# Chunked attention with memory and an MLP on one core: moving the copies of memory rows from GpSimd to VectorE, and re-ordering the front

## The chip, the cores and the metric

One NeuronCore of a Trainium2 chip. The time is that of the device for one execution, in microseconds (us). The engines are named as in the profile: PE is TensorE (PEld its loading of weights), DVE is VectorE, ACT is ScalarE, POOL is GpSimd, SP is SyncE, which here only issues transfers. The kernel before takes 242.05 us (median of three runs, 241.57 to 242.69).

## The reference, cut to what matters

Four batches, eight heads, 768 positions, heads of 64. Queries come in chunks of 32; a chunk sees 16 keys to the left, its own 32, 8 to the right, and 8 memory keys. What comes out is normalised, goes through an MLP of 512 to 2048 to 512 with relu, and is added to itself.

```python
chunk, left_ctx, right_ctx = (32, 16, 8)
for c in range(nc):
    c_start = c * chunk; c_end = c_start + chunk
    l_start = max(0, c_start - left_ctx); r_end = min(S, c_end + right_ctx)
    k_full = np.concatenate([mem_k, k[:, :, l_start:r_end]], axis=2)
    v_full = np.concatenate([mem_v, v[:, :, l_start:r_end]], axis=2)
    scores = scale * np.matmul(q[:, :, c_start:c_end], k_full.transpose(0, 1, 3, 2))
    a = np.exp(scores - np.max(scores, axis=-1, keepdims=True))
    a = a / (np.sum(a, axis=-1, keepdims=True) + 1e-09)
    out[:, :, c_start:c_end] = np.matmul(a, v_full)
...                                   # x: out with the heads side by side, 512 wide
xn = (x - mu) / np.sqrt(var + 1e-06) * g_ln
return x + np.maximum(xn @ w_ch1, 0.0) @ w_ch2
```

## The kernel before

The work is cut into 24 tiles of 128 positions (six for each batch), and these into eight units of three tiles for the MLP. The order of all instructions is written by hand: a prologue, then a plan of 28 steps for each unit `u`. In steps 0 to 15 stands one `up` projection each, in 16 to 27 one part of a `down` projection each; `at(u, step, ...)` puts other work behind a step.

Values are kept in groups of 64 positions: `V` has 104 rows (96 of context, 8 of memory) for each of 12 groups, and two buffers for even and odd batches. The 8 memory rows are the same in every group, so they are copied within SBUF from `memv16`. Keys are kept transposed in `KT` in the same groups, with the memory keys as columns 96 to 103.

```python
att = [ps.tile([128, 2, 512], FP32, ...) for i in range(2)]   # PSUM, two banks each
mm = [ps.tile([128, 512], FP32, ...) for i in range(4)]       # PSUM, one bank each

def v_mem(b, g0, g1, eng):           # 8 rows, g1 - g0 groups of 640 elements
    src = memv16[96:W, b, :, :]
    copy(eng, free(V[b % 2][96:W, g0:g1, :, :], 0, [[H * VW, g1 - g0], [1, H * VW]]),
         bass.AP(tensor=src.tensor, offset=src.offset,
                 ap=[list(src.ap[0]), [0, g1 - g0], [1, H * VW]]))

def key_piece(b, src, g, first, lo, n, eng, half=None):   # PSUM -> KT, one group
    ...
def pieces(b, blk, banks, phase):
    for n in range(2):
        key_piece(b, banks[phase], 4 * blk + n, *PIECES[n], dve, phase)
        key_piece(b, banks[1 - phase], 4 * blk + 2 + n, *PIECES[2 + n], act, 1 - phase)

def turn_keys(b, blk):               # 8 transposes on PE, then the first pieces
    p = slot("att")
    banks = [as16(p[:, h, :]) for h in range(2)]
    block_slot[b, blk] = banks
    transpose_block(b, blk, 0, banks)
    pieces(b, blk, banks, 0)
def more_keys(b, blk):
    pieces(b, blk, block_slot[b, blk], 1)
    edges(b, blk, dve)
def turn_queries(b, blk):            # 8 transposes, two copies on ACT
    ...
def mix(b, blk, which, eng):         # re-orders a loaded block for the transposes
    ...
def cross(b, blk, which):            # batches 2 and 3: transposed by DMA instead of PE
    ...
    nc.sync.dma_start_transpose(out=o, in_=i)
def norm(b, t):                      # xn = (x - mean) * g
    nc.vector.scalar_tensor_tensor(out=xn[i % 4], in0=xs[i % 9], scalar=nmean[t], in1=gb, ...)
def turn_x(b, t):                    # transposes xn into xT: PE in units 0 and 1, then DMA
    ...
def up(u, hc, lo=0, n=3):            # 4 matmuls of 128x384 into one bank of mm, then a relu
    p = slot("mm")[:, 0 : 128 * n]
    ...
    relu(act if hc % 2 else dve, rT[c][:, i, 128 * lo : 128 * (lo + n)], p)
def up_tile(u, c, i, eng):           # the same for one tile: 16 matmuls of 128x128
    ...
```

The first block of keys and queries is loaded in fp32 and cast by VectorE and ScalarE (`mix_raw`); all other loads are issued by GpSimd and cast on the way. The prologue and the plan, as far as they are spoken of:

```python
for which in range(2):               # first block: keys, then queries
    for par in range(2):
        nc.sync.dma_start(out=raws[which][par], in_=dram((k, q)[which], ...))
nc.scalar.dma_start(out=memkf, in_=dram(mem_k, ...))
nc.scalar.dma_start(out=grow, in_=dram(moe_g_ln, ...))
load_mem_v(0, nc.scalar)
...
load_w1(1)
v_mem(0, 2, 6, pool)
load_block(0, 1, 1)
...
warm(6)                              # matmuls on zeros
p = slot("att")
nc.tensor.matmul(out=p[:, 0, :], lhsT=gone, rhs=grow, start=True, stop=True)  # gain, fp32
...
scores(0, 0)
v_mem(0, 0, 2, dve)
...
at(0, 13, v_mem, 0, 6, NG, pool)
at(1, 0, turn_keys, 1, 0)
at(1, 0, v_mem, 1, 0, 4, dve)
at(1, 1, more_keys, 1, 0)
at(1, 2, turn_queries, 1, 0)
at(1, 4, v_mem, 1, 4, NG, pool)
...
for b in (2, 3):
    for i in range(3):
        at(w, 8 + i, v_mem, b, 4 * i, 4 * i + 4, pool)
```

Of the kernel before, what the change touches and what calls it, by code (L numbers as in the profile page):

```python
# [15 lines left out]
def kernel(  # L16
# [80 lines left out]
    def as16(t):  # L97
        return t.bitcast(FP16)

    def copy(eng, out, in_):  # L100
        if eng is nc.scalar:
            eng.copy(out=out, in_=in_)  # L102
        else:
            eng.tensor_copy(out=out, in_=in_)  # L104
# [27 lines left out]

    def v_mem(b, g0, g1, eng):
# [39 lines left out]
    def key_piece(b, src, g, first, lo, n, eng, half=None):  # L173

        h, m = (0, 8) if half is None else (4 * half, 4)
        copy(eng, free(KT[b % 2], GW * g + 16 + 8 * lo + h, [[W, 4], [8, n], [1, m]]),
             free(src, 4 * (first + lo), [[1, 4], [4, n], [128, m]]))
# [16 lines left out]
            key_piece(b, banks[phase], 4 * blk + n, *PIECES[n], dve, phase)  # L194
            key_piece(b, banks[1 - phase], 4 * blk + 2 + n, *PIECES[2 + n], act, 1 - phase)

    def first_pieces(b, blk, banks, k0):

        for n in range(2):
            key_piece(b, banks[n], 4 * blk + k0, *PIECES[k0], dve, n)  # L200
            key_piece(b, banks[1 - n], 4 * blk + k0 + 1, *PIECES[k0 + 1], act, 1 - n)

    def edges(b, blk, eng):
        if blk:
# [11 lines left out]
            )  # L216

    def turn_keys(b, blk):
        p = slot("att")
        banks = [as16(p[:, h, :]) for h in range(2)]  # L220
        block_slot[b, blk] = banks
        transpose_block(b, blk, 0, banks)
        pieces(b, blk, banks, 0)
# [207 lines left out]


    raws = ((osb[0], osb[1]), (osb[2], xs[4]))
    for which in range(2):
        for par in range(2):
            nc.sync.dma_start(
                out=raws[which][par],
                in_=dram((k, q)[which], 4 * par * HS, [[512, 32], [HS, 4], [1, 512]]),
            )

    def load_mem_v(b, eng):
        eng.dma_start(
            out=xs[5 + b][96:W, :], in_=dram(mem_v, b * 4096, [[64, 8], [512, 8], [1, 64]])
        )

    nc.scalar.dma_start(out=memkf, in_=dram(mem_k, 0, [[64, 128], [128 * 64, 2], [1, 64]]))
    nc.scalar.dma_start(out=grow, in_=dram(moe_g_ln, 0, [[512, 1], [1, 512]]))
    load_mem_v(0, nc.scalar)

    PAIR = 1.0 / 128 + 15.0 / 2**20  # L450

    def ones(i, g0, g1, eng):

        eng.memset(V[i].bitcast(FP32)[:, g0:g1, :, 32:40], PAIR)
# [12 lines left out]
    def mem_vals(b):  # L467
        copy(act, memv16[96:W, b, :, 0:64], xs[5 + b][96:W, :].rearrange("p (h d) -> p h d", h=8))

    make_identity(nc, identity)  # L470
    nc.vector.memset(zero, 0.0)
    nc.vector.memset(gone, 1.0)
    ones(0, 0, 2, dve)
    nc.vector.memset(V[0][0:32, 0, :, :], 0.0)
    clear_keys(0, dve)
    nc.vector.memset(mhalf, -0.5)
    nc.vector.memset(memv16.bitcast(FP32)[96:W, :, :, 32:40], PAIR)
    ones(0, 2, NG, dve)
    copy(dve, memk16, memkf)
    total(band[:, 0:1], 56, 96)  # L480
    total(band[:, 1:2], 0, 32)
    total(cnt[:, 2:3], 88, 96)
    nc.vector.tensor_tensor(out=band[:, 1:2], in0=band[:, 1:2], in1=cnt[:, 2:3], op=ALU.add)
    nc.vector.tensor_scalar(out=band, in0=band, scalar1=NEG, scalar2=None, op0=ALU.mult)

    mem_vals(0)
    load_v(0, 0)
    load_v(0, 1)
    load_block(0, 1, 0)
# [1 line left out]
    load_v(0, 2)  # L491
    load_v(0, 3)
    load_w1(1)
    v_mem(0, 2, 6, pool)
    load_block(0, 1, 1)
    load_w1(2)
    load_v(0, 4)
# [8 lines left out]
    nc.gpsimd.memset(V[1][0:32, 0, :, :], 0.0)  # L506
    nc.gpsimd.memset(V[1][64:96, NG - 1, :, :], 0.0)
    load_block(0, 2, 1)
    load_w2(1)
    clear_keys(1, pool)  # L510
    load_v(0, 8)
    load_v(0, 9)
    load_w2(2)
    load_v(0, 10)
    load_v(0, 11)
    load_w2(3)

    warm(6)
    p = slot("att")
    nc.tensor.matmul(out=p[:, 0, :], lhsT=gone, rhs=grow, start=True, stop=True)  # L520
    gp = p
    mem_keys()
    warm(1)
    K0 = [as16(mm[0]), as16(mm[1])]
    Q0 = [as16(mm[2]), as16(mm[3])]
    mix_raw(0, raws[0], 0, dve)
    mix_raw(0, raws[0], 1, act)
    transpose_block(0, 0, 0, K0)
    mix_raw(1, raws[1], 0, dve)
    mix_raw(1, raws[1], 1, act)  # L530
    first_pieces(0, 0, K0, 0)
    transpose_block(0, 0, 1, Q0)
    mem_cols(0, dve)
    copy(act, gb, gp[:, 0, :])
    quarter_q(0, 0, 0, Q0)
    warm(1, 512, gp[:, 1, :])
    scores(0, 0)
    v_mem(0, 0, 2, dve)
    soften(0, 0, 0)
    soften(0, 0, 1)  # L540
    mix(0, 1, 0, dve)
    first_pieces(0, 0, K0, 2)
    quarter_q(0, 0, 1, Q0)
    transpose_block(0, 1, 0, K0)
    total(cnt[:, 0:1], 16, 128)
    count_v(0, 0, 0)
    values(0, 0)
    first_pieces(0, 1, K0, 0)
    key_right(0, 3, dve)
    norm(0, 0)  # L550
    scores(0, 1)
    soften(0, 1, 0)
    soften(0, 1, 1)
    warm(2, 512, mm[2])
    turn_x(0, 0)
    values(0, 1)
    turn["mm"] = 2
    up_tile(0, 0, 0, act)
    norm(0, 1)
    first_pieces(0, 1, K0, 2)  # L560
    key_left(0, 4, dve)
    mix(0, 1, 1, dve)
    up_tile(0, 1, 0, act)
    turn_x(0, 1)
    transpose_block(0, 1, 1, K0)
    quarter_q(0, 1, 0, K0)
    quarter_q(0, 1, 1, K0)
    up_tile(0, 0, 1, act)
    scores(0, 2)
    soften(0, 2, 0)  # L570
    up_tile(0, 1, 1, dve)
    soften(0, 2, 1)
# [3 lines left out]
    up_tile(0, 2, 0, dve)  # L576
    values(0, 2)
    up_tile(0, 2, 1, act)
    norm(0, 2)
    mix(0, 2, 0, dve)  # L580
    up_tile(0, 3, 0, act)
    up_tile(0, 3, 1, act)
    turn_x(0, 2)
    mix(0, 2, 1, dve)
    plan = {}

    def at(u, step, fn, *args):
# [34 lines left out]
        load_block(b, blk, 0)  # L622
        load_block(b, blk, 1)

    at(0, 13, v_mem, 0, 6, NG, pool)
    order = [(load_pair, (0,))] + [(load_v, (g,)) for g in range(4)]
    order += [(load_pair, (1,)), (mem_cols, (pool,)), (load_v, (4,)), (load_v, (5,))]
    order += [(load_pair, (2,))] + [(load_v, (g,)) for g in range(6, 12)]
# [3 lines left out]
    at(0, 26, count_v, 1, 1, NG - 1)  # L632
    at(0, 24, mix, 1, 0, 0, dve)
    at(0, 26, mix, 1, 0, 1, dve)
    at(1, 0, turn_keys, 1, 0)
    at(1, 0, v_mem, 1, 0, 4, dve)
    at(1, 1, more_keys, 1, 0)
    at(1, 2, mix, 1, 1, 0, dve)
    at(1, 2, turn_queries, 1, 0)
    attend(6, 3, 7, 1)  # L640
    at(1, 4, v_mem, 1, 4, NG, pool)
    at(1, 4, mix, 1, 1, 1, dve)
    at(1, 6, turn_keys, 1, 1)
    at(1, 7, more_keys, 1, 1)
    at(1, 9, turn_queries, 1, 1)
    attend(7, 9, 13, 1)
    attend(8, 12, 16, 1)
    at(1, 15, mix, 1, 2, 0, dve)
    at(1, 19, turn_keys, 1, 2)
    at(1, 20, more_keys, 1, 2)  # L650
    at(1, 20, mix, 1, 2, 1, dve)
    at(1, 23, turn_queries, 1, 2)

    for b in (2, 3):
        u = 2 * b - 1
        w = u - 1
        for blk in range(3):
            at(w - 1, 23 + blk, load_pair, b, blk)
        at(w, 0, mem_cols, b, pool)
        for g in range(NG):  # L660
            at(w, 1 + g // 2, load_v, b, g)
        for i in range(3):
            at(w, 8 + i, v_mem, b, 4 * i, 4 * i + 4, pool)
# [64 lines left out]
```

## Time and profile before

| what | measured |
|---|---|
| time, median of three runs | 242.05 us |
| span of the profiled execution | 241.3 us |
| PE busy | 217.1 us (90%) |
| DVE busy | 133.9 us (55%) |
| ACT busy | 105.7 us (44%) |
| POOL busy | 117.3 us (49%) |
| PE busy in 0 to 80 us | 60.8 us |
| mean granted clock of PE | 0.969 |

The page gives busy times for the whole span; with PE at 90% they don't say which part of the span could be shorter. For that it has a line for each engine in which each digit stands for a fortieth of the span (6 us), in tenths, and one for the clock granted to PE. A table of shorter stretches gives the same in us, with the number of instructions in brackets. The timeline lists instructions in order of time; in brackets it has how long the engine was idle before, and which instruction ended that idle time. Line numbers are those of the kernel; L104 is the copy helper, so all copies of VectorE and GpSimd bear it and are told apart by their tiles.

### The profile page before, as it was taken

How to read it: one execution, taken by the hardware profiler on the slowest of the kernel's cores; microseconds unless marked ns; L12 is line 12 of the kernel's file. 1: busy time of each engine (PE TensorE's matmuls, PEld its weight loads, DVE VectorE, ACT ScalarE, POOL GpSimd, SP SyncE). 2: the span in 40 equal slices, each digit the busy share in tenths (PEclk: the TensorE clock that was granted, in tenths of full speed). 3: DMA queues.
4: the chain of work that ended last, by engine and by line, in shares of the span. 5: the costliest groups of instructions: out<-in, count | busy, mean ns of one | idle time of the engine just before them, and what ended most of it. 6: DMA issues, size and time to landing. Idle time of an engine off the chain costs nothing.

```text
span 241.3 us, 4939 instructions
## 1 busy us (share of the span) xinstructions
PE 217.1 (90%) x1944; PEld 133.3 (55%) x1944; DVE 133.9 (55%) x320; ACT 105.7 (44%) x220; POOL 117.3 (49%) x173
## 2 busy tenths in 40 slices
PE   8557859899678999999999999997999999999993
PEld 2245758554445645664566457643674467446653
DVE  5656293249836663679657436773475257515221
ACT  3543521855155832773387207732674057203300
POOL 7987696998700077899401387699111101200000
PEclk9999995999959999999999999999999999999999
DMA  6999999999300169999951299999911311221012
GB/s 173 183 196 196 199 198 196 169 146 78 119 0 3 22 84 182 220 130 152 175 148 24 65 166 204 125 132 173 210 42 22 109 46 24 43 87 43 3 43 87
DMA packets 72857, 27.85 MB, mean 115 GB/s; under 512 B 60929, under 2 KB 68865, under 8 KB 72834
## 3 DMA queue, kind: packets, MB, share of 16 engines
q0 software_dynamic: 45632, 14.56, 58.5%
q1 hardware_dynamic: 26856, 12.90, 25.8%
q8 instruction: 15, 0.25, 0.4%
q10 hardware_dynamic: 346, 0.08, 0.2%
q14 instruction: 8, 0.07, 0.1%
HBM read 30.28 MB, written 6.29 MB: 152 GB/s over the span
## 4 chain that ended last, share of the span: by engine, by line
PE 67%; DMA 16%; POOL 8%; DVE 5%; issue 2%; ACT 1%; DVEq 0%
PE mm L366 30%; PE mm L392 27%; PE att L279 4%; DMA w2c<-in_moe_w_ch_dram 4%; DMA w1c<-in_moe_w_ch_dram 4%; DMA st<-in_q_dram 3%; DMA xT<-xn 3%; PE att L300 3%; POOL st L120 3%; POOL V L128 2%; PE mm L414 1%; DVE KT L104 1%; DVE V L104 1%; DMA V<-in_v_dram 1%; POOL V L104 1%
## 5 line engine op out<-in xcount | busy, mean ns | idle before, releaser
L392 PE MATMUL mm<-w2c,rT 128*128 128x512 f16 x368 | 82.6, 379 | 0.0
L366 PE MATMUL mm<-xT,w1c 128*128 128x384 f16 x448 | 80.2, 332 | 1.8 <-DMA xT<-xn 1.3
L366 PEld LDWEIGHTS <-w1c 128*128 128x128 f16 x448 | 49.3, 115 | 25.5 <-issue 2.5
L392 PEld LDWEIGHTS <-rT 128*128 128x128 f16 x368 | 34.9, 98 | 40.0
L360 DVE TENSOR_SCALAR rT<-mm 128x384 f16<-128x384 f32 (+1 forms) x60 | 33.9, 564 | 33.1 <-PE mm L366 28.2
L358 ACT ACTIVATE rT<-mm 128x384 f16<-128x384 f32 (+1 forms) x64 | 32.3, 505 | 42.1 <-PE mm L366 19.0
L289 ACT ACTIVATE AT<-att,band 104x512 f16<-104x512 f32 x48 | 31.3, 685 | 28.8 <-PE att L279 28.6
L331 POOL TENSOR_SCALAR veps<-sq 128x1 f32<-128x1 f32 x24 | 5.6, 235 | 73.4 <-ACT junk L325 40.1
L128 POOL DMA_DIRECT2D V<-in_v_dram x48 | 37.5, 786 | 7.5 <-issue 3.4
L401 DVE SCALAR_TENSOR_TENSOR osb<-mm,rstd,xs 128x512 f32<-128x512 f32 x23 | 17.2, 749 | 30.6 <-PE mm L392 28.3
L104 POOL COPY V<-memv 8x2560 f16<-8x2560 f16 (+2 forms) x9 | 25.4, 2842 | 0.9 <-DVE V L104 0.7
L325 ACT ACTIVATE junk<-xs,nmean 128x512 f16<-128x512 f32 x24 | 17.3, 720 | 12.9 <-DVE nmean L314 12.9
L320 DVE SCALAR_TENSOR_TENSOR xn<-xs,nmean,gb 128x512 f16<-128x512 f32 x24 | 22.1, 922 | 0.4
L279 PE MATMUL att<-QR,KT 64*104 64x64 f16 x384 | 16.5, 237 | 5.2 <-ACT QR L102 3.7
L279 PEld LDWEIGHTS <-KT 64*104 64x104 f16 x384 | 13.0, 137 | 9.2 <-issue 6.1
L308 DVE SCALAR_TENSOR_TENSOR xs<-att,rec 128x512 f32<-128x512 f32 x24 | 16.6, 692 | 0.8
L377 PE MATMUL mm<-xT,w1c 128*128 128x128 f16 x192 | 14.5, 242 | 2.6 <-ACT KT L102 1.2
L377 PEld LDWEIGHTS <-w1c 128*128 128x128 f16 x192 | 13.6, 122 | 3.1 <-issue 2.9
L335 POOL TENSOR_TENSOR rstd<-veps,mhalf 128x1 f32<-128x1 f32 x24 | 14.3, 597 | 2.0
L102 ACT COPY KT<-rawk 128x352 f16<-128x352 f16 (+1 forms) x12 | 8.8, 791 | 11.7 <-DMA rawk<-iv 11.7
L120 POOL DMA_DIRECT2D st<-in_k_dram x22 | 12.6, 590 | 2.0 <-DMA st<-in_k_dram 1.0
L120 POOL DMA_DIRECT2D st<-in_q_dram x22 | 12.4, 579 | 2.4 <-DMA st<-in_q_dram 1.3
(74 smaller groups left out, 146.6 us busy)
## 6 DMA issues: line engine op xcount, KB each, us to landing
out_dram<-osb SPq DMA_DIRECT2D x23, 256.0 KB, 2.1
V<-in_v_dram POOLq DMA_DIRECT2D x40, 96.0 KB, 8.1
st<-in_k_dram POOLq DMA_DIRECT2D x22, 128.0 KB, 5.9
st<-in_q_dram POOLq DMA_DIRECT2D x22, 128.0 KB, 6.5
w1c<-in_moe_w_ch_dram POOLq DMA_DIRECT2D x4, 512.0 KB, 9.4
w2c<-in_moe_w_ch_dram POOLq DMA_DIRECT2D x4, 512.0 KB, 9.2
V<-in_v_dram POOLq DMA_DIRECT2D x8, 80.0 KB, 7.4
osb<-in_k_dram SPq DMA_DIRECT2D x2, 256.0 KB, 3.5
```

Of the source, the lines that this page charges most:

```text
L104: eng.tensor_copy(out=out, in_=in_)
L120: nc.gpsimd.dma_start(out=s[:, 512 * par : 512 * par + 512], in_=dram((k, q)[which], (b * H + 4 * par) * HS + blk * 256 * D, [[512, 32], [ ...
L128: nc.gpsimd.dma_start(out=V[b % 2][lo:hi, g, :, 0:64], in_=dram(v, b * H * HS + (64 * g - 16 + lo) * D, [[64, hi - lo], [HS, H], [1, 64]]),)
L279: nc.tensor.matmul(out=p[0:W, par, (4 * gg + j) * 64 : (4 * gg + j) * 64 + 64], lhsT=KT[b % 2][rows, 2 * t + gg, j, :], rhs=free(QR[b % 2] ...
L289: nc.scalar.activation(out=free(AT[t % 3], 32 * c, [[64, 16], [1, 32]]), in_=free(p, 4 * c, [[64, 16], [1, 4], [8, 8]], W), func=ACTF.Exp, ...
L320: nc.vector.scalar_tensor_tensor(out=xn[i % 4], in0=xs[i % 9], scalar=nmean[t], in1=gb, op0=ALU.add, op1=ALU.mult,)
L325: nc.scalar.activation(out=junk, in_=xs[(NT * b + t) % 9], func=ACTF.Square, bias=nmean[t], scale=1.0, accum_out=sq[t],)
L358: nc.scalar.activation(out=o, in_=p, func=ACTF.Relu)
L360: nc.vector.tensor_scalar(out=o, in0=p, scalar1=0.0, scalar2=None, op0=ALU.max)
L366: nc.tensor.matmul(out=p, lhsT=free(w1c[c][:, dt, :], i, [[4, 128]]), rhs=xT[u % 2][:, dt, 128 * lo : 128 * (lo + n)], start=(dt == 0), st ...
L377: nc.tensor.matmul(out=p[:, 128 * k_ : 128 * k_ + 128], lhsT=free(w1c[c][:, dt, :], k_, [[4, 128]]), rhs=xT[u % 2][:, dt, 128 * i : 128 * ...
L392: nc.tensor.matmul(out=p, lhsT=rT[c][:, k_, 128 * i : 128 * i + 128], rhs=w2c[c][:, k_, :], start=(c == 0 and k_ == 0), stop=(c == 3 and k ...
```

## The change

It has four parts.

1. The memory rows of values of batches 0 and 1 are copied by VectorE, in pieces of two or four groups at places of their own; GpSimd copies those of batches 2 and 3 as before. In return GpSimd clears and fills the constant columns of the first V buffer ahead of its first loads.
2. The two transfers of the first queries are issued by ScalarE's queue, beside those of the keys on SyncE's. The small transfers (memory keys, gain, memory values) move to SyncE's queue, behind the keys.
3. `turn_keys` transposes into two of the four one-bank tiles instead of one two-bank tile.
4. The front is re-ordered: the gain's matmul comes after the first scores, the pieces of keys of the first two blocks are written one group at a time, projections of ready tiles stand earlier; a few steps of the plan shift, among them the DMA transposes of keys and queries in batches 2 and 3, which come later.

```diff
-    def first_pieces(b, blk, banks, k0):
-        for n in range(2):
-            key_piece(b, banks[n], 4 * blk + k0, *PIECES[k0], dve, n)
-            key_piece(b, banks[1 - n], 4 * blk + k0 + 1, *PIECES[k0 + 1], act, 1 - n)
+    def window(b, blk, banks, k0, eng):
+        for half in ((0, 1) if eng is dve else (1, 0)):
+            key_piece(b, banks[half], 4 * blk + k0, *PIECES[k0], eng, half)
 ...
     def turn_keys(b, blk):
-        p = slot("att")
-        banks = [as16(p[:, h, :]) for h in range(2)]
+        banks = [as16(slot("mm")) for _ in range(2)]
 ...
-    for which in range(2):
+    for which, eng in ((0, nc.sync), (1, nc.scalar)):
         for par in range(2):
-            nc.sync.dma_start(
+            eng.dma_start(
 ...
-    nc.scalar.dma_start(out=memkf, ...)
-    nc.scalar.dma_start(out=grow, ...)
-    load_mem_v(0, nc.scalar)
+    nc.sync.dma_start(out=memkf, ...)
+    nc.sync.dma_start(out=grow, ...)
+    load_mem_v(0, nc.sync)
 ...
     make_identity(nc, identity)
+    nc.gpsimd.memset(V[0][0:32, 0, :, :], 0.0)
+    ones(0, 0, NG, pool)
 ...
-    ones(0, 0, 2, dve)
-    nc.vector.memset(V[0][0:32, 0, :, :], 0.0)
-    ones(0, 2, NG, dve)
-    copy(dve, memk16, memkf)           # before the small reductions; now after them
 ...
-    v_mem(0, 2, 6, pool)
 ...                                    # prologue: V loads 8, 9 ahead of w2 chunk 1
+    v_mem(0, 2, 4, dve)                # after soften(0, 1)
 ...
+    v_mem(0, 4, 6, dve)                # after soften(0, 2)
 ...
-    at(0, 13, v_mem, 0, 6, NG, pool)
+    at(0, 13, v_mem, 0, 6, 8, dve)
+    at(0, 16, v_mem, 0, 8, NG, dve)
 ...
+    at(0, 27, v_mem, 1, 0, 4, dve)
     at(1, 0, turn_keys, 1, 0)
-    at(1, 0, v_mem, 1, 0, 4, dve)
     at(1, 1, more_keys, 1, 0)
-    at(1, 2, turn_queries, 1, 0)
-    attend(6, 3, 7, 1)
-    at(1, 4, v_mem, 1, 4, NG, pool)
+    at(1, 1, turn_queries, 1, 0)
+    attend(6, 4, 8, 1)
-    at(1, 9, turn_queries, 1, 1)
-    attend(7, 9, 13, 1)
-    attend(8, 12, 16, 1)
+    at(1, 10, turn_queries, 1, 1)
+    at(1, 11, v_mem, 1, 4, 8, dve)
+    attend(7, 11, 14, 1)
+    attend(8, 13, 17, 1)
+    at(1, 15, v_mem, 1, 8, NG, dve)
 ...
-                at(w, (7, 16, 21)[blk] + 3 * which, cross, b, blk, which)
+                at(w, (7, 18, 23)[blk] + 3 * which, cross, b, blk, which)
-        at(w, 24, spread, b, 1, dve, act)
-        at(u, 6, spread, b, 2, dve, act)
+        at(w, 27, spread, b, 1, dve, act)
+        at(u, 9, spread, b, 2, dve, act)
```

More of the change, by code (lines that the diff above doesn't have):

```diff
@@ L444, in load_mem_v @@
         )
-    nc.scalar.dma_start(out=memkf, in_=dram(mem_k, 0, [[64, 128], [128 * 64, 2], [1, 64]]))
-    nc.scalar.dma_start(out=grow, in_=dram(moe_g_ln, 0, [[512, 1], [1, 512]]))
-    load_mem_v(0, nc.scalar)
+    nc.sync.dma_start(out=memkf, in_=dram(mem_k, 0, [[64, 128], [128 * 64, 2], [1, 64]]))
+    nc.sync.dma_start(out=grow, in_=dram(moe_g_ln, 0, [[512, 1], [1, 512]]))
+    load_mem_v(0, nc.sync)
     PAIR = 1.0 / 128 + 15.0 / 2**20
@@ L484 @@
     nc.vector.tensor_scalar(out=band, in0=band, scalar1=NEG, scalar2=None, op0=ALU.mult)
-    mem_vals(0)
+    copy(dve, memk16, memkf)
     load_v(0, 0)
@@ L508 @@
     load_block(0, 2, 1)
+    load_v(0, 8)
+    load_v(0, 9)
     load_w2(1)
     clear_keys(1, pool)
-    load_v(0, 8)
-    load_v(0, 9)
-    load_w2(2)
     load_v(0, 10)
     load_v(0, 11)
+    load_w2(2)
     load_w2(3)
     warm(6)
[L519 to L523, printed above, removed]
     K0 = [as16(mm[0]), as16(mm[1])]
@@ L527 @@
     mix_raw(0, raws[0], 1, act)
+    mem_keys()
     transpose_block(0, 0, 0, K0)
@@ L530 @@
     mix_raw(1, raws[1], 1, act)
-    first_pieces(0, 0, K0, 0)
+    window(0, 0, K0, 0, dve)
+    window(0, 0, K0, 1, act)
     transpose_block(0, 0, 1, Q0)
     mem_cols(0, dve)
-    copy(act, gb, gp[:, 0, :])
     quarter_q(0, 0, 0, Q0)
-    warm(1, 512, gp[:, 1, :])
+    mem_vals(0)
     scores(0, 0)
-    v_mem(0, 0, 2, dve)
     soften(0, 0, 0)
     soften(0, 0, 1)
+    window(0, 0, K0, 2, dve)
+    p = slot("att")
+    nc.tensor.matmul(out=p[:, 0, :], lhsT=gone, rhs=grow, start=True, stop=True)
+    copy(act, gb, p[:, 0, :])
+    window(0, 0, K0, 3, act)
+    quarter_q(0, 0, 1, Q0)
     mix(0, 1, 0, dve)
-    first_pieces(0, 0, K0, 2)
-    quarter_q(0, 0, 1, Q0)
-    transpose_block(0, 1, 0, K0)
+    v_mem(0, 0, 2, dve)
     total(cnt[:, 0:1], 16, 128)
@@ L547 @@
     values(0, 0)
-    first_pieces(0, 1, K0, 0)
+    transpose_block(0, 1, 0, K0)
+    norm(0, 0)
+    window(0, 1, K0, 0, dve)
     key_right(0, 3, dve)
-    norm(0, 0)
+    window(0, 1, K0, 1, act)
+    warm(1, 512, mm[2])
+    turn_x(0, 0)
     scores(0, 1)
@@ L553 @@
     soften(0, 1, 1)
-    warm(2, 512, mm[2])
-    turn_x(0, 0)
-    values(0, 1)
+    v_mem(0, 2, 4, dve)
     turn["mm"] = 2
     up_tile(0, 0, 0, act)
+    window(0, 1, K0, 2, dve)
+    window(0, 1, K0, 3, act)
+    key_left(0, 4, dve)
+    values(0, 1)
     norm(0, 1)
-    first_pieces(0, 1, K0, 2)
-    key_left(0, 4, dve)
+    warm(1, 512, mm[2])
     mix(0, 1, 1, dve)
@@ L564 @@
     turn_x(0, 1)
-    transpose_block(0, 1, 1, K0)
-    quarter_q(0, 1, 0, K0)
-    quarter_q(0, 1, 1, K0)
+    Q1 = [as16(slot("mm")) for _ in range(2)]
+    transpose_block(0, 1, 1, Q1)
+    quarter_q(0, 1, 0, Q1)
     up_tile(0, 0, 1, act)
@@ L570 @@
     soften(0, 2, 0)
+    soften(0, 2, 1)
+    quarter_q(0, 1, 1, Q1)
+    v_mem(0, 4, 6, dve)
     up_tile(0, 1, 1, dve)
-    soften(0, 2, 1)
+    up_tile(0, 2, 0, dve)
+    values(0, 2)
+    norm(0, 2)
+    up_tile(0, 2, 1, act)
+    mix(0, 2, 0, dve)
+    up_tile(0, 3, 0, act)
+    up_tile(0, 3, 1, dve)
+    turn_x(0, 2)
+    mix(0, 2, 1, dve)
     total(cnt[:, 1:2], 0, 80)
@@ L575 @@
     nc.vector.tensor_tensor(out=cnt[:, 1:2], in0=cnt[:, 1:2], in1=cnt[:, 2:3], op=ALU.add)
[L576 to L584, printed above, removed]
     plan = {}
@@ L650 @@
     at(1, 20, more_keys, 1, 2)
-    at(1, 20, mix, 1, 2, 1, dve)
+    at(1, 18, mix, 1, 2, 1, dve)
     at(1, 23, turn_queries, 1, 2)
```

## The prediction, made before the changed kernel had run

> **What bounds the kernel now.** I read the busy line of the page first. TensorE (PE) is busy for 217.1 of 241.3 us, and from 80 us on it hardly stops (a table of stretches gives 20.00 of 20 us again and again). What can be won lies before 80 us, where PE is busy for 60.8 of 80 us. The slices (6 us each) show where:
>
> ```profile
> PE   8557859899678999999999999997999999999993
> ...
> POOL 7987696998700077899401387699111101200000
> PEclk9999995999959999999999999999999999999999
> DMA  6999999999300169999951299999911311221012
> ```
>
> PE is loose in slices 0 to 7 and 10 to 12, and the granted clock has two dips, one right after each of two idle spells. The DMA engines are full up to about 40 us; this will limit how far the front can be pulled in. The table of 2 us stretches places the dips (columns: PE, PEld, DVE, ACT, POOL busy, then PEclk):
>
> ```profile
> 32.00:34.00 2.00, 1.37 (x25) 1.21 (x22) 1.97 (x2) 1.41 (x3) 2.00 (x1) 1.00 1.84 179
> 34.00:36.00 2.00, 0.02 (x1) 0.03 (x2) 2.00 (x2) 0.00 (x1) 2.00 (x3) 0.85 1.21 206
> 36.00:38.00 2.00, 1.42 (x13) 1.25 (x14) 1.01 (x3) 0.00 (x0) 1.78 (x4) 0.50 1.77 184
> ...
> 64.00:66.00 2.00, 0.08 (x1) 0.00 (x0) 1.97 (x2) 0.00 (x0) 1.15 (x1) 1.00 0.00 0
> 66.00:68.00 2.00, 0.25 (x7) 0.40 (x9) 1.41 (x4) 1.38 (x4) 0.00 (x0) 0.53 0.00 0
> 68.00:70.00 2.00, 2.00 (x20) 1.25 (x19) 0.00 (x0) 1.85 (x4) 0.00 (x0) 0.50 0.00 0
> ```
>
> While PE stands still, DVE and POOL each work at one or two instructions. The timeline names them (start, length, engine, line). First spell:
>
> ```profile
> 31.99 3.38 POOL L104 COPY V<-memv 8x3840 f16<-8x3840 f16 x1
> 32.10 3.81 DVE L320 SCALAR_TENSOR_TENSOR xn<-xs,nmean,gb 128x512 f16<-128x512 f32 x1
> 35.98 0.60 PE L348 MATMUL att<-identity,xn 128*128 128x128 f16 x4 [2.61 <-DVE xn L320]
> ```
>
> The norm on VectorE takes 3.81 us here and about 0.75 elsewhere; it ends just after GpSimd's copy of mem rows does. PE waits 2.61 us for it. Second spell:
>
> ```profile
> 60.64 4.52 POOL L104 COPY V<-memv 8x5120 f16<-8x5120 f16 x1 [0.74 <-DVE V L104]
> ...
> 62.22 0.31 ACT L102 COPY KT<-att 128x176 f16<-128x176 f16 x1 [3.54 <-DVE KT L104]
> 62.55 0.34 DVE L104 COPY KT<-att 128x176 f16<-128x176 f16 x1 [0.37 <-ACT KT L102]
> ...
> 62.92 2.91 DVE L104 COPY V<-memv 8x2560 f16<-8x2560 f16 x1
> ...
> 67.75 0.90 PE L279 MATMUL att<-QR,KT 64*104 64x64 f16 x16 [3.68 <-ACT QR L102]
> ...
> 68.59 4.03 PE L366 MATMUL mm<-xT,w1c 128*128 128x384 f16 x12
> ...
> 77.90 2.14 PE L366 MATMUL mm<-xT,w1c 128*128 128x384 f16 x12
> ```
>
> VectorE's own copy of four groups is held until 65.83, behind it the pieces of keys, behind these ScalarE's copies of queries, and PE waits 3.68 us. Then twelve matmuls take 4.03 us, which at the full clock take 2.14. A third, smaller spell is at 8.05: GpSimd's copy of 2.32 us, beside it a cast of VectorE that takes 1.99 us instead of 0.29, and PE 2.33 us idle.
>
> **What the Trainium skill says.** (1) "GPSIMD Engine Reference", 8 Key points: GpSimd shares its SBUF interfaces with VectorE, with contention against two-port modes and two SBUF inputs. The trace agrees: the norm and SBUF-to-SBUF copies are held (3.81, 2.91, 1.99 us), while in 60.64 to 62.9 copies out of PSUM keep their 0.30 to 0.34 us. (2) "TensorE: Matmul & The Clock Gate", Part 1: after an idle window of about 3.4 us PE falls to half clock and needs about as long to return. The trace shows 0.50 for about 6 us after each spell. (3) "PSUM — Partial Sum Buffer", the section on bank collisions: two engines may not use one bank at once, so software orders them. In the trace the pieces from the two-bank tile att alternate (61.88, 62.22, 62.55, 62.93), though they use different banks; at 22.86, from two one-bank tiles, two pieces on each engine run side by side in 0.66 us. (4) "DMA: Bandwidth & Descriptors", the section saying that issuing engines are not separate queues: only issue time is saved by a second issuer. Each raw load costs about 0.6 us of issue here.
>
> **The change, part by part.**
>
> *Mem rows.* Three of GpSimd's nine copies go: 2.32 + 3.38 + 4.52 = 10.2 us. VectorE gets, by the row of 0.49 us for 8x1280 (two groups) and an estimate of 0.82 for 8x2560 (0.33 for each further two groups, from the free-running 0.49 less about 0.16 of fixed cost): batch 0 three times 0.49 and once 0.82, batch 1 twice 0.82, so 3.9 us. It is given back 3.06 (norm), 2.09 (copy) and 1.70 (cast) of stalls, 6.85 us. All new copies stand where VectorE has room, except the one of 0.82 us just ahead of the first relu of the second unit.
>
> *Spell at 32 us.* The idle time of 2.61 and 0.58 us goes, and with it the slow clock: 16 up matmuls took 1.86 us against 1.05, 32 took 3.16 against 1.98, 8 transposes 1.06 against 0.61, 4 took 0.60 against 0.39; 2.65 us in all. Before it PE waits 1.24, 0.46 and 0.73 us for evacuations (22 to 27 us); the re-ordered front spreads these, I take half, 1.2. Some of the norm's wait stays. Walking the new order with the lengths of the trace from the first scores to the first down projection, I get 5.9 us less.
>
> *Spell at 64 us.* 3.68 us of idle time, 2.39 of slow clock (1.89 of the twelve matmuls, 0.25 of scores, 0.25 of eight transposes) and most of the 1.05 us wait for keys at 76.78. Eight pieces in pairs take about 1.3 us where the alternating ones took 2.7 without the stall. Against it: the keys now hold two of the four banks that the up projections use, so an up waits for the pieces; with the copy of 0.82 us ahead I see two waits of 0.6 us, and some more later. Net 5.5.
>
> *Front.* Queries are issued beside the keys, not 1.3 us behind; GpSimd's first loads start about 0.5 us later (two memsets, 0.62 and 0.74 us, go ahead of them). The last query half lands at 8.5 us now; I expect about 6.8. The mem keys, first on their queue before, are now third, and VectorE waits for them before its first cast; keys suffer a little. With the 1.7 us stall gone, the first scores should start near 9.8 instead of 12.12: 2.3 us. The gain row's product (2.07 us of PE) moves behind the first scores and lies beside the softmax.
>
> *Later.* The transposes of keys by DMA come after those of xn in two units. The 1.28 us wait of PE at 168.46 for xT should go: 1.3.
>
> Sum: 5.9 + 5.5 + 2.3 + 1.3 = 15.0. Such walks see no wait that appears anew, and nearly all PE time between 10 and 65 us would have to be filled; I take 2.5 off. 242.05 - 12.5 = 229.5.
>
> **Rivals.** *Transfers become the bound of the front.* The DMA engines run full at about 196 GB/s to 40 us; query block 2 lands at 31.1 and the last chunk of w2 at 41.05, whatever the engines do. The new order wants that block near 30 and that chunk near 47, so it should just fit; if not, VectorE stands at the mix and half of the 5.9 is lost: about 232.5. *The banks become the bound.* Four key blocks take two of four banks; should each cost the ups 1 us more, 233.5. For it: relus and pieces queue on the same two engines. Against it: PE needs 0.65 us for an up, a relu 0.55. *VectorE becomes the bound.* It is busy 4.6 of 5 us in 55 to 65 us; but much of this is the stall itself. About 232. *The front gains nothing*, because keys and queries share the engines and mem keys come later: 231.8.
>
> **Range and chances.** The rival of the banks in full (4.0) and that of the transfers by half (1.5) give 235; the full walk without my deduction gives 227, and a little less if the ups fill better. Range 225.5 to 235. To miss 2% (237.2) two thirds of the sum must fail, while the two stalls are direct in the trace: faster 0.93, same 0.05, slower 0.02.
>
> **What would show it.** In the changed profile: no DVE norm or cast over 1 us before 80 us; copies V<-memv on DVE near 0.5 and 0.8 us; PEclk without the dips in slices 5 and 6, 10 to 12; first scores near 9.8; pieces of keys in pairs; first down near 36 instead of 44.7, second unit at about 52 instead of 60.4; no wait for xT near 156. The prediction is wrong if a dip stays, if PE waits for DMA or for relus of ups beside key blocks, or if the first scores start after 11.

## The result and the profile after

The changed kernel takes **231.36 us** (median of four executions, 229.9 to 233.87) against 242.19 us for the kernel before in the same runs: ratio 0.953, 95% interval 0.948 to 0.959, or 10.8 us less. The prediction was 229.5 us with a range of 225.5 to 235.

The profiled execution took 233.87 us, the longest of the four; where it matters, the profile of a second run of the same kernel (229.3 us) is given beside it.

First the page of the changed kernel, the same lines as were shown of the kernel before (slices of 5.8 us):

```profile
PE   4789989955999999999999999997999999999993
...
POOL 8967755799311668599211965579112002100000
PEclk9999999997699999999999999999999999999999
DMA  6999999999501699998911799999913203211012
```

Counted from 0 as in the prediction, PE is dense from slice 3 to 7, and the two dips of the clock of the kernel before are gone (its clock row has them in slices 6 and 11). In slices 8 and 9 (46 to 58 us) there is a hole in PE, and a new dip of the clock in 9 and 10. This is not the old spell moved forward: the timeline of the changed kernel shows that there are no held copies and norms in this part any more. These are three instructions of VectorE up to 40 us (start, length, engine, line, output and input):

```profile
34.00 0.49 DVE L104 COPY V<-memv 8x1280 f16<-8x1280 f16 x1
...
35.68 0.82 DVE L104 COPY V<-memv 8x2560 f16<-8x2560 f16 x1
...
39.80 0.75 DVE L318 SCALAR_TENSOR_TENSOR xn<-xs,nmean,gb 128x512 f16<-128x512 f32 x1
```

The moved copies take 0.49 and 0.82 us on VectorE, the lengths that the prediction reckoned with; the norm takes 0.75 us. What stands in the hole is another thing. The timeline of the changed kernel at the start of the second unit, GpSimd (POOL) between VectorE and PE:

```profile
48.30 1.10 POOL L120 DMA_DIRECT2D st<-in_q_dram  x2
...
49.73 0.57 POOL L333 TENSOR_TENSOR rstd<-veps,mhalf 128x1 f32<-128x1 f32 x1
50.27 1.64 POOL L128 DMA_DIRECT2D V<-in_v_dram  x2
50.34 0.75 DVE L399 SCALAR_TENSOR_TENSOR osb<-mm,rstd,xs 128x512 f32<-128x512 f32 x1 [2.18 <-POOL rstd L333]
...
52.26 0.56 POOL L333 TENSOR_TENSOR rstd<-veps,mhalf 128x1 f32<-128x1 f32 x1
...
52.86 0.75 DVE L399 SCALAR_TENSOR_TENSOR osb<-mm,rstd,xs 128x512 f32<-128x512 f32 x1 [1.63 <-POOL rstd L333]
53.52 0.41 DVE L351 COPY xT<-att 128x512 f16<-128x512 f16 x1
...
53.99 0.81 PE L364 MATMUL mm<-xT,w1c 128*128 128x384 f16 x4 [4.48 <-DVE xT L351]
```

Read from the bottom: by its own records PE has finished the first unit at about 49.5 and waits 4.48 us for xT. VectorE could have copied xT long before, but in its list the two outputs `osb` of the first unit stand ahead, and each waits for its `rstd`, the reciprocal square root that GpSimd computes. `rstd` is 0.57 us of work; it is late because in GpSimd's list each `root` (the pair `veps`, `rstd`) stands behind loads of keys, queries and values: GpSimd is busy for 1.8 to 2.0 of every 2 us from 46 to 56 us, mostly with issuing these loads (two loads of values take it 1.64 us here). In the kernel before the three `rstd` start at nearly the same times (49.64, 52.17 and 54.64 us, here 49.73, 52.26 and 55.11), but the first `osb` only began at 58.50 us:

```profile
52.17 0.57 POOL L335 TENSOR_TENSOR rstd<-veps,mhalf 128x1 f32<-128x1 f32 x1
...
54.64 0.56 POOL L335 TENSOR_TENSOR rstd<-veps,mhalf 128x1 f32<-128x1 f32 x1
...
58.50 0.75 DVE L401 SCALAR_TENSOR_TENSOR osb<-mm,rstd,xs 128x512 f32<-128x512 f32 x1
```

The change thus moved forward what needs `rstd`, and not `rstd` itself. Behind the wait PE runs at half clock for about 3 us in the second profile, and for some 7 us in this one.

Milestones from the timelines (us; the changed kernel in both profiles; in brackets the figure of the longer execution):

| | before | changed | changed, second profile |
|---|---|---|---|
| first scores | 12.12 | 9.91 | 9.91 |
| first down projection | 44.69 | 35.38 | 35.73 |
| PE done with unit 1 (start of the next less its wait) | 59.94 | 49.51 | 49.87 |
| second unit starts | 60.42 | 53.99 | 53.24 |
| from there to the end of the span | 180.9 | (178.1) | 174.3 |

So PE is done with the first unit 10 us earlier, but starts the second only 6.4 to 7.2 us earlier: 2.9 to 4.0 us were given back at once. From that start to the end the second profile gains another 6.6 us.

VectorE's stalls are not all gone. GpSimd still copies the rows of batches 2 and 3, and a norm beside them takes 2.80 us. The line of the timeline, and below it the stretch from 100 to 108 us (columns: PE, PEld, DVE, ACT, POOL busy, then the clock):

```profile
100.27 2.80 DVE L318 SCALAR_TENSOR_TENSOR xn<-xs,nmean,gb 128x512 f16<-128x512 f32 x1
```

```profile
100.00:108.00 8.00, 8.00 (x39) 3.63 (x37) 7.93 (x7) 2.20 (x5) 7.86 (x5) 1.00 1.61 151
```

PE is busy for 8.00 of these 8.00 us: a held instruction costs nothing here, because PE does not wait for it.

### The profile page after: what moved, and what is told of

Its sections match the earlier page's. It is cut to its first block, busy times and chain, and to the rows that moved or that the text cites. A ratio compares the mean times of both kernels' runs of the same rounds, so it can differ in the third digit from the quotient of the medians.

```text
span 232.1 us, 4947 instructions
## 1 busy us (share of the span) xinstructions
PE 214.6 (92%) x1942; PEld 131.1 (56%) x1942; DVE 134.8 (58%) x324; ACT 103.9 (45%) x219; POOL 111.0 (48%) x172
## 4 chain that ended last, share of the span: by engine, by line
PE 81%; DMA 6%; DVE 4%; POOL 3%; ACT 2%; issue 1%; SPq 1%; DVEq 0%; ACTq 0%
PE mm L364 32%; PE mm L390 29%; PE att L277 6%; PE mm L375 5%; DMA rawk<-iv 5%; PE att L298 4%; DMA memkf<-in_mem_k_dram 2%; PE mm L212 2%; POOL V L128 2%; PE mm L412 2%; PE att L212 1%; POOL st L120 1%; DVE xs L306 1%; PE att L533 1%; POOL rstd L333 1%
## 5 line engine op out<-in xcount | busy, mean ns | idle before, releaser
L364 PEld LDWEIGHTS <-w1c 128*128 128x128 f16 x448 | 49.4, 115 | 31.4 <-issue 9.6
L356 ACT ACTIVATE rT<-mm 128x384 f16<-128x384 f32 (+1 forms) x63 | 31.6, 505 | 37.2 <-PE mm L364 19.2
L128 POOL DMA_DIRECT2D V<-in_v_dram x48 | 39.0, 818 | 16.1 <-DMA V<-in_v_dram 4.0
L318 DVE SCALAR_TENSOR_TENSOR xn<-xs,nmean,gb 128x512 f16<-128x512 f32 x24 | 20.0, 833 | 0.5
L277 PE MATMUL att<-QR,KT 64*104 64x64 f16 x384 | 16.0, 235 | 0.5 <-ACT QR L102 0.5
L333 POOL TENSOR_TENSOR rstd<-veps,mhalf 128x1 f32<-128x1 f32 x24 | 15.4, 641 | 2.0
L104 DVE COPY iv<-st 128x1024 f16<-128x1024 f16 x22 | 13.1, 594 | 2.7 <-DMA QR<-iv 1.8
L104 POOL COPY V<-memv 8x2560 f16<-8x2560 f16 x6 | 14.4, 2434 | 0.1
L375 PE MATMUL mm<-xT,w1c 128*128 128x128 f16 x192 | 13.3, 231 | 0.9 <-DVE xT L351 0.9
```

Of the source, the lines that this page charges most:

```text
L128: nc.gpsimd.dma_start(out=V[b % 2][lo:hi, g, :, 0:64], in_=dram(v, b * H * HS + (64 * g - 16 + lo) * D, [[64, hi - lo], [HS, H], [1, 64]]),)
L277: nc.tensor.matmul(out=p[0:W, par, (4 * gg + j) * 64 : (4 * gg + j) * 64 + 64], lhsT=KT[b % 2][rows, 2 * t + gg, j, :], rhs=free(QR[b % 2] ...
L356: nc.scalar.activation(out=o, in_=p, func=ACTF.Relu)
L364: nc.tensor.matmul(out=p, lhsT=free(w1c[c][:, dt, :], i, [[4, 128]]), rhs=xT[u % 2][:, dt, 128 * lo : 128 * (lo + n)], start=(dt == 0), st ...
L375: nc.tensor.matmul(out=p[:, 128 * k_ : 128 * k_ + 128], lhsT=free(w1c[c][:, dt, :], k_, [[4, 128]]), rhs=xT[u % 2][:, dt, 128 * i : 128 * ...
```

## The experiments

Theories after the result. **T**: the change works by ending the stalls of VectorE beside GpSimd's copies and by pairing the pieces of keys, and its gain is cut by the roots that stand behind loads. **Rivals**: the gain comes from the re-ordered front and queues, not from the copies; the hole at 50 us is made by the pairs of banks or by the slow clock; the end of the transfers sets it anyway. Medians are given; "before" is the kernel before in the same set of runs. Of its 33 timed executions, 30 took 240.84 to 243.97 us, but three took 234.59, 235.79 and 236.92 us; none of these was profiled, why they were shorter is open, and beside them the changed kernel gains some 5 us and not 11.

### The roots ahead of the loads

```diff
-        at(0, 19 + t, root, 0, t)
+        at(0, 16, root, 0, t)
```

> The changed kernel with one thing moved: the small chain for 1/std of the first three tiles (two short GpSimd instructions each) is put at step 16 of unit 0, ahead of most loads of batch 1 in GpSimd's list, not at steps 19 to 21 between them. In the profile of the changed kernel the first output (DVE osb) waits 2.18 us for GpSimd's rstd, VectorE's copy of xT stands behind two such outputs, PE waits 4.48 us for xT at 53.99 and another 1.03 at 56.51, and its clock then falls to half for some 7 us. Theory (the gain was won by 49 us and partly given back to a new wait on GpSimd's list): the second unit starts near 50 instead of 53.99, no dip, 5.5 us of idle time and about 2.7 us of slow clock go; 222.5 to 225. Rival (transfers of batch 1 are the true bound, and rstd only stands in the same queue): PE then waits at 50 to 60 us for the blocks or values of batch 1, and the time is 229 or more.

Measured: 226.28 us (225.69 to 226.7), before 242.73; ratio 0.935 (0.929 to 0.940). The timeline of this run at the same place:

```profile
48.65 0.74 DVE L399 SCALAR_TENSOR_TENSOR osb<-mm,rstd,xs 128x512 f32<-128x512 f32 x1
...
50.11 0.41 DVE L351 COPY xT<-att 128x512 f16<-128x512 f16 x1
...
50.43 4.26 POOL L128 DMA_DIRECT2D V<-in_v_dram  x5
...
50.57 0.81 PE L364 MATMUL mm<-xT,w1c 128*128 128x384 f16 x4 [0.48 <-DVE xT L351]
```

The wait for `rstd` is gone, the second unit starts 2.7 to 3.4 us earlier, and no slow clock follows there. The loads still stand in the list, now behind the roots, and no wait of PE for a load follows. The cause of the hole is settled: the place of three small operations in GpSimd's list. The gain fell short of what I expected by 1.3 us at least. I had counted the slow clock as a loss on top of the wait; the run with a warm PE below shows that ending it brings nothing by itself.

### The copies back on GpSimd, all else changed

```diff
+    v_mem(0, 2, 6, pool)                     # in GpSimd's list where it was
-    v_mem(0, 2, 4, dve)
-    v_mem(0, 4, 6, dve)
 ...
-    at(0, 13, v_mem, 0, 6, 8, dve)
-    at(0, 16, v_mem, 0, 8, NG, dve)
+    at(0, 13, v_mem, 0, 6, NG, pool)
-    at(1, 11, v_mem, 1, 4, 8, dve)
-    at(1, 15, v_mem, 1, 8, NG, dve)
+    at(1, 4, v_mem, 1, 4, NG, pool)
```

> The changed kernel with part 1 alone undone: memory rows of batches 0 and 1 copied by GpSimd in its old pieces (groups 2 to 5 in the prologue, 6 to 11 at step 13, groups 4 to 11 of batch 1 at step 4 of unit 1), all else as changed. Theory (GpSimd's copies hold VectorE's work within SBUF): VectorE norms, casts or copies of over 1.5 us appear beside each of the three copies, while copies out of PSUM keep 0.3 us; GpSimd's loads come 2 to 4 us later as well, and the roots with them; 236 to 240. Rival (the order and the banks made the gain, the copies only lay where VectorE had room): 230 to 233.

Measured: 235.03 us (233.57 to 236.31), ratio 0.970 (0.964 to 0.977): the changed kernel loses 3.7 us of its gain. The time lies just under the range that T gave, and above that of the rival. The stall is back in the timeline of this run, in a place that shows what it is made of:

```profile
32.75 3.42 POOL L104 COPY V<-memv 8x3840 f16<-8x3840 f16 x1
...
33.17 3.01 DVE L584 TENSOR_TENSOR cnt<-cnt 128x1 f32<-128x1 f32 x1
36.11 0.54 DVE L104 COPY KT<-mm 128x144 f16<-128x144 f16 x2
...
37.23 1.05 PE L375 MATMUL mm<-xT,w1c 128*128 128x128 f16 x16 [2.67 <-ACT KT L102]
```

An addition of one element for each partition, which takes 0.16 us elsewhere, lasts 3.01 us and ends with GpSimd's copy. Behind it stand the pieces of keys, and PE waits 2.67 us. The victim is thus not the norm as such: here it is an addition, in the kernel before also copies and casts within SBUF (2.91 and 1.99 us). The 3.7 us hold one thing more. In the changed order the memory values are prepared later, so GpSimd stands 2.03 us for them, starts its first copy at 10.51 us (8.05 in the kernel before), and issues the next load at 13.09 us (8.44 in the changed kernel).

### The copies alone moved, in the kernel before

The same edit the other way round, in the kernel before:

```diff
-    v_mem(0, 2, 6, pool)
+    v_mem(0, 2, 6, dve)                      # behind soften(0, 1, 1)
-    at(0, 13, v_mem, 0, 6, NG, pool)
+    at(0, 13, v_mem, 0, 6, 8, dve)
+    at(0, 16, v_mem, 0, 8, NG, dve)
-    at(1, 4, v_mem, 1, 4, NG, pool)
+    at(1, 11, v_mem, 1, 4, 8, dve)
+    at(1, 15, v_mem, 1, 8, NG, dve)
```

> The kernel before with part 1 alone done: the same rows copied by VectorE in pieces at the places of the changed kernel's plan; order, queues and banks as before. Theory: both clock dips (34 to 42 us, 66 to 72 us) go, the front gains 1.7 us by the cast that is no longer held; in sum 233 to 236, of which part may be given back to GpSimd's roots as in the changed kernel. Rival (the re-ordered front makes most of the gain): 238 to 241.

Measured: 235.41 us (234.87 to 237.13), ratio 0.973 (0.967 to 0.979): 7.3 us less by the copies alone. The first scores start at 10.43 us instead of 12.12, the second unit at 55.10 instead of 60.42. What stays is the wait for queries behind alternating pieces, 3.0 us, at the start of the second unit. By the run just before, the rest of the change without the copies brings 7.7 us; both together brought 10.8, not 15.0. The two halves overlap in the hole at 50 us, where whoever comes early waits for the roots: with the roots early, both together bring 16.4.

### The two-bank tile for keys back: with the roots late, then early

```diff
-        banks = [as16(slot("mm")) for _ in range(2)]
+        p = slot("att")
+        banks = [as16(p[:, h, :]) for h in range(2)]
```

> The changed kernel with part 3 alone undone: keys of the third block of batch 0 and of batch 1 transposed into one two-bank tile again, so pieces of keys on VectorE and ScalarE alternate. Theory (the pairs save 1.3 us for each of four blocks, a part of it on the path): pieces at 0.35 us one after the other, PE waits near the second unit's start and at its step 6; 232 to 234. Rival (two of the four banks taken from the up projections cost as much as the pairs gain): 229.5 to 231.5.

> The kernel with the early roots (226.28 us), and in it part 3 alone undone (keys in one two-bank tile of att). In the changed kernel undoing it cost nothing (231.58 against 231.36), but there the second unit began at 53.8 in both, held by GpSimd's rstd. Theory (the pairs are worth something, hidden there by the later wait): pieces alternate at 0.35 us, eight of them take 2.7 us in place of 1.3, the first scores of unit 1 start 1.5 to 2.5 us later after its start, and PE waits; 228 to 230. Rival (the banks taken from the up projections cost what the pairs gain): 225.5 to 227.

Measured on the changed kernel: 231.58 us (230.82 to 232.44), no difference. Its profile shows how the later wait covers the loss: PE is done with the first unit 1.5 us later than in the second profile of the changed kernel (51.35 against 49.87), then waits 2.44 us for xT instead of 3.37, and starts the second unit at 53.79 us, between the 53.24 and 53.99 of the changed kernel. (PE's wait of 2.31 us for queries behind alternating pieces comes after that; why it leaves no mark in the time isn't shown.) That left the worth of the pairs open, so I tried it again where the hole is closed: with the roots early it takes 229.79 us (227.48 to 229.97) against 226.28, **3.5 us**. Both medians are of different sets of runs, but three other kernels with early roots in the set of the 229.79 took 226.31 to 226.86. The profiled execution is the shortest of the six (227.48), so its timeline shows only 1.8 us of the loss. The timeline of this second run:

```profile
55.24 0.29 ACT L102 COPY KT<-att 128x160 f16<-128x160 f16 x1 [0.41 <-DVE KT L104]
...
55.56 0.31 DVE L104 COPY KT<-att 128x144 f16<-128x144 f16 x1 [0.36 <-ACT KT L102]
...
55.91 0.30 ACT L102 COPY KT<-att 128x176 f16<-128x176 f16 x1
...
57.45 0.65 PE L278 MATMUL att<-QR,KT 64*104 64x64 f16 x16 [1.66 <-ACT QR L102]
```

One engine's piece begins where the other's ends, in turn; the scores come 6.0 us after the unit's start. With one-bank tiles and early roots the same pieces are two groups on ScalarE (0.50 us each) and one of four on VectorE (1.01 us), and the scores come 5.2 us after the start (50.57 to 55.81). The first run shows how a sound part can look worthless while a later wait covers it.

### Queues, mem keys, and the transposes by DMA, with the roots early

Three parts undone one by one; each against 226.28 us. First, all raw loads on SyncE's queue and the mem keys on ScalarE's, as before:

```diff
-    for which, eng in ((0, nc.sync), (1, nc.scalar)):
+    for which, eng in ((0, nc.sync), (1, nc.sync)):
...
-    nc.sync.dma_start(out=memkf, ...)        # and grow, load_mem_v(0)
+    nc.scalar.dma_start(out=memkf, ...)
```

> The kernel with the early roots (226.28 us), with part 2 alone undone: first queries on SyncE's queue behind the keys, mem keys, gain and mem values on ScalarE's. Theory (the earlier queries pull in the first scores): first scores later by 0.5 to 1 us; 226.8 to 227.5. Rival (the 16 engines are full, so the queries only take from the keys, and the mem keys, third in their queue now, hold VectorE until 6.4 us): first scores at the same time within 0.3 us or earlier; 225.5 to 226.7.

Measured: 226.31 us (225.98 to 227.34). No difference: the first scores start at 9.62 us, while in the profiles with queries on ScalarE's queue they start at 9.91 (changed kernel) and 10.69 (roots early). The rival holds. The Trainium skill ("DMA: Bandwidth & Descriptors", issuing engines are not separate queues) says that a second issuer saves issue time only, and this run agrees. On ScalarE's queue the last half of the queries lands 3.9 us after its issue at 1.39 us (changed kernel), on SyncE's 5.0 us after 2.71. But the second half of the keys is then cast at 6.08 us instead of 4.72 and the mem keys at 6.43 instead of 2.60, so that VectorE casts the last queries at 7.75 us in one and at 7.78 in the other. What the queries gain, the keys and mem keys lose. The front varies by itself, too: with the same order of loads the first scores start between 9.79 and 10.69 us in the profiles.

Second, the cast of mem keys and their transposes behind the first keys:

```diff
-    copy(dve, memk16, memkf)
     ...
     mix_raw(0, raws[0], 0, dve)
+    copy(dve, memk16, memkf)
     ...
-    mem_keys()
     transpose_block(0, 0, 0, K0)
+    mem_keys()
```

> The kernel with the early roots (226.28 us), with the cast of mem keys behind VectorE's casts of the first keys, and their transposes behind those of the first keys. Theory (VectorE stands at the mem keys until they land at 6.4 while the keys have landed): PE's first transposes start near 6.6 and not 7.4, first scores 0.3 to 0.7 us earlier; 225.5 to 226. Rival (queries land last and set the first scores): no change, 226.0 to 226.6.

Measured: 226.45 us (225.89 to 227.45), no gain. VectorE no longer waits for the mem keys, but the first scores still begin only at 10.34 us, because ScalarE's half of the raw queries, cast behind its copies of mem keys, then holds the last transposes by 0.83 us. Moving the wait of 3.1 us for the mem keys out of the way is not enough as long as ScalarE's casts of the queries stand behind its copies of the mem keys.

Third, the transposes by DMA at their old steps:

```diff
-                at(w, (7, 18, 23)[blk] + 3 * which, cross, b, blk, which)
+                at(w, (7, 16, 21)[blk] + 3 * which, cross, b, blk, which)
-        at(w, 27, spread, b, 1, dve, act)
-        at(u, 9, spread, b, 2, dve, act)
+        at(w, 24, spread, b, 1, dve, act)
+        at(u, 6, spread, b, 2, dve, act)
```

> The kernel with the early roots (226.28 us), with the DMA transposes of keys and queries of batches 2 and 3 and the pieces that follow them at their old steps. Theory: they stand ahead of the last transpose of xn in SyncE's queue again, and PE waits 1.3 to 2 us for xT near 150 us (1.28 us in the kernel before, 2.0 in the run with the copies alone); 227.3 to 228.5. Rival (the wait came from loads that lie elsewhere now): no such wait, 225.8 to 226.8.

Measured: 226.86 us (225.86 to 229.98), 0.6 more than 226.28 and within the spread. Its profile has one wait of 0.67 us for xT by DMA, where I expected 1.3 to 2; that with the new steps has none of 0.2 us or more. By these runs this part is worth 0.6 us or nothing.

### PE kept warm through the wait

```diff
     at(0, 27, v_mem, 1, 0, 4, dve)
+    at(0, 27, warm, 16, 512, att[0][:, 1, :])   # 16 matmuls of zeros
```

> The changed kernel, with 16 matmuls on zeros put on PE ahead of the second unit, where it waits 4.48 us for xT. They leave the wait as it is and only keep PE at work, some 3.5 us of it. Theory (an idle spell costs twice, by itself and by the half clock after it): the up projections and transposes after 54 us run at the full clock (12 of 128x384 in 2.1 us, not 3.64), the second unit starts at the same time, and the time falls by 2 to 2.7 us, to 228.7 to 229.4. Rival (the slow clock lies beside waits for VectorE and GpSimd that end at the same time anyway): within 0.7 us of 231.36.

> The changed kernel once more, beside the three others on one chip, for comparison with the one with matmuls on zeros and the best one. Theory: as before, 230.5 to 232, with PE's wait of 3 to 5 us ahead of the second unit and the dip of its clock. Rival (that wait was a matter of one execution): no such wait in this profile, and 228 or less.

Measured: 231.22 us (230.81 to 232.07), and the unchanged kernel beside it 230.80 (229.3 to 231.99). No gain, though the clock did stay up, as the timeline of the warm run shows:

```profile
49.40 3.62 PE L428 MATMUL att<-zero 128*128 128x512 f16 x16
...
54.06 0.81 PE L364 MATMUL mm<-xT,w1c 128*128 128x384 f16 x4 [1.04 <-DVE xT L351]
...
56.59 0.81 PE L364 MATMUL mm<-xT,w1c 128*128 128x384 f16 x4 [1.27 <-DVE osb L399]
```

The ups take 0.81 us (1.44 in the second profile of the unchanged kernel) and the transposes 0.61 (1.06). PE reaches the next wait sooner and stands there for 1.27 us (0.24 in the second profile), for `osb`, which again waits for `rstd`. The slow clock cost nothing here, because PE was not what the others waited for.

### GpSimd's copies cut, not moved

In the kernel before, each of the three copies cut into pieces of two groups, all on GpSimd:

```diff
-    v_mem(0, 2, 6, pool)
+    v_mem(0, 2, 4, pool)
+    v_mem(0, 4, 6, pool)
-    at(0, 13, v_mem, 0, 6, NG, pool)
+    for i in range(3):
+        at(0, 13, v_mem, 0, 6 + 2 * i, 8 + 2 * i, pool)
-    at(1, 4, v_mem, 1, 4, NG, pool)
+    for i in range(4):
+        at(1, 4, v_mem, 1, 4 + 2 * i, 6 + 2 * i, pool)
```

> The kernel before, with GpSimd's three copies cut into pieces of two groups (2 + 3 + 4 pieces of 8x1280 for pieces of 4, 6 and 8 groups); same engine, same places, same bytes. Theory A (VectorE is held until GpSimd's list leaves a gap, so the pieces one behind the other hold it as long as the whole): the norm beside them still takes over 3 us, 241 to 243. Theory B (it is held until the end of one instruction): the norm takes about 0.75 us and up to one piece more, 1.0 to 2.0 us, both idle spells of PE shrink below 2 us and the clock dips go; 235 to 239.

Measured: 235.49 us (235.04 to 236.26), about the same as by moving them (235.41, in another set). Moving the copies also takes some 10 us of work off GpSimd; cutting them leaves it all there. So the gain comes from VectorE being held less, not from GpSimd having less to do. The timeline, GpSimd and VectorE:

```profile
31.48 4.29 POOL L104 COPY V<-memv 8x1280 f16<-8x1280 f16 x3
...
31.11 0.75 DVE L320 SCALAR_TENSOR_TENSOR xn<-xs,nmean,gb 128x512 f16<-128x512 f32 x1
31.78 1.48 DVE L104 COPY iv<-st 128x1024 f16<-128x1024 f16 x1
33.19 0.41 DVE L353 COPY xT<-att 128x512 f16<-128x512 f16 x1
33.52 1.14 DVE L104 COPY iv<-st 128x1024 f16<-128x1024 f16 x1
```

GpSimd copies for 4.29 us, longer than the 3.38 of the whole copy, and no instruction of VectorE is held for more than about one piece: 1.48 and 1.14 us for what takes 0.43 alone, while `xT` out of PSUM passes in 0.41. VectorE is held until **one** instruction of GpSimd ends, not until GpSimd rests. The norm itself was not put to the test: it starts 0.37 us ahead of GpSimd's first piece and takes its 0.75 us. The wait for queries behind alternating pieces stays (2.98 us), as with the copies moved (2.99).

### A version that draws on all this

The roots early; the mem keys first on ScalarE's queue, so that VectorE has them early; the copy of 0.82 us away from the start of the second unit:

```diff
-        at(0, 19 + t, root, 0, t)
+        at(0, 16, root, 0, t)
-    nc.sync.dma_start(out=memkf, ...)
+    nc.scalar.dma_start(out=memkf, ...)      # ahead of the raw loads
-    at(0, 27, v_mem, 1, 0, 4, dve)
+    at(1, 3, v_mem, 1, 0, 4, dve)
```

> The kernel with the early roots, and two moves more: mem keys first on ScalarE's queue, ahead of the queries, and VectorE's copy of mem rows for groups 0 to 3 of batch 1 from ahead of the first relu of unit 1 to step 3. Theory (VectorE stands for the mem keys until they land, and PE waits 0.47 us for that relu): mem keys land near 3.2, first scores near 9.0, no wait at the relu; 225.0 to 225.9. Rival (both are hidden behind other waits): 226.0 to 226.6.

Measured: **224.46 us** (223.78 to 225.14), beside 230.80 for the changed kernel and 241.79 for the kernel before in the same set: the fastest here. Against roots early alone (226.28, another set) it is 1.8 us less. The cast of mem keys is done at 2.8 us, the first scores start at 8.85, the second unit at 49.81, and no up of that unit waits for a relu. The mem keys and the copy were moved in one run; which of them brought how much wasn't tried apart.

## Why the prediction was right

The time fell within the range, 1.9 us above the point. The direction and the main cause, GpSimd's copies that hold VectorE, were right; that the point came so near is in part luck, since errors of both signs cancel. Step by step:

- *Mem rows.* Right. The added copies measured 0.49 and 0.82 us where that was the estimate, no norm or cast over 1 us is left before 80 us, and the copies alone bring 7.3 us.
- *Spell at 32 us (5.9) and front (2.3).* Together 8.2 predicted; PE is done with the first unit 10.1 to 10.4 us earlier, so these two were too small by about 2 us. First scores at 9.91 (9.8 predicted), first down at 35.38 (36). But the working of the front was wrong in one term: the queue of the queries brings nothing (226.31 against 226.28), and the copies alone already gain 1.7 of the 2.2 us.
- *Start of the second unit.* The step that failed. The prediction put it at about 52 us and saw there only two waits of 0.6 us for banks. PE was free at 49.5 to 49.9, but stood 3.4 to 4.5 us for xT behind `osb` behind `rstd`. GpSimd's list was read for its copies and not for the small operations behind loads, although the profile before shows the three `rstd` ending at 50.2, 52.7 and 55.2 us, around the predicted start.
- *Spell at 64 us (5.5) and later (1.3).* The sum fits: behind the start of the second unit the second profile is 6.6 us shorter. The pairs of pieces are there and worth 3.5 us where no later wait covers them. The later part alone is too large: undoing it costs 0.6 us at most by the medians, and while the second profile of the changed kernel has no wait for xT by DMA near 156 us, the longer execution still has one of 0.38 us at 158. What the slow clock in the kernel before cost by itself was not tested.
- *The 2.5 taken off for waits not seen.* The right idea in too small a size: the root wait alone cost 4.5 to 5.1 us (230.80 or 231.36 less 226.28). With it gone, the kernel stands 16.4 us under its kernel before (242.73), near the 15.0 of the walk without the deduction.
- *Signs of being wrong.* One of them came: a dip of the clock stays. It is a new one, behind the root wait, and goes with it.
- *Rivals.* Banks as the bound: one wait of 0.47 us for a relu in the second unit with the roots early; taking the pairs back loses time, so this rival falls. Transfers: it came true in another form than I wrote it, for VectorE does not stand at the mix; GpSimd's queue of loads holds what stands behind it. VectorE as the bound: its share of the span rises from 58% in the changed kernel to 62% with the roots early, and that kernel is faster, so it falls. Front gains nothing: half true, of its queue part only.

## What to carry to other kernels

Where one engine both issues loads and computes, read its list for small operations that stand behind loads, and compare when they end now with when they will be needed: a kernel made faster ahead of them meets them as a new wait (here about 5 us for three operations of 0.8 us), and a place ahead of the loads ends it. Look for one instruction of another engine that grows to the length of a GpSimd instruction beside it, and for PE waiting behind it; move or cut the latter, whichever is simpler. Where PE does not wait, as from 100 to 108 us here, leave it. And when undoing a part shows no loss, ask first whether a later wait covers it: the same part measured 0.2 us with the wait and 3.5 us without.

## What the runs showed of the hardware that I had not expected

- A VectorE operation of one element for each partition is held as long as a wide one: 0.16 us became 3.01 beside a GpSimd copy of 8 partitions. The Trainium skill ("GPSIMD Engine Reference", 8 Key points) names two SBUF inputs as a case of contention, and this addition has two; that so small an operation waits as long, and that the hold ends with the one instruction, comes from these traces.
- Cutting GpSimd's copy of 8x3840 into three costs GpSimd 0.9 us (4.29 against 3.38), and the kernel gains about as much as by moving the copies.
- The granted clock on the page can differ where PE's speed does not. From 8 to 20 us it is 0.50 in the run with queues as before and 1.00 in the profile of the changed kernel, yet sixteen matmuls of 128x128 near 17 us take 1.90 us in both (1.05 at 30 us). Executions of that run with mean clocks of 0.966 and 1.000 took 226.26 and 226.31 us. The lengths of like matmuls are the surer sign here.
- In the kernel before, PE is already at half clock after an idle spell of 2.61 us (four transposes at 35.98 us take 0.60 us instead of 0.39), shorter than the idle window of about 3.4 us that the prediction goes by.
